# Window attention with its gradients: weight gradients in 64x64 array tiles between md and attention, scores two quads ahead

## The chip, the cores and the metric

One core of one Trainium2 chip. The metric is the device time of one execution in us; lower is better. Fast runs of one kernel mostly agree within 0.3%. A profile gives a trace of the engines: PE (TensorE matmul), PEld (its weight loads), DVE (VectorE), ACT (ScalarE), POOL (GpSimd), SP (SyncE, which issues DMA). Times read in the trace count from the start of the span, which is about 2 us shorter than the metric.

## The reference

Attention in 8x8 windows of a 256x256 image with 384 channels (one head), its output, and the gradients of x, wqkv and wo:

```
xw  = x in windows of 64 tokens                       # 1024 windows
q, k, v = split(xw @ wqkv)
p   = softmax(q k^T * C**-0.5)
o   = (p @ v) @ wo                                    # out_0
grads = vjp(f, x, wqkv, wo)(grad_out)                 # out_1, out_2, out_3
```

## The kernel before

The kernel handles eight windows at a time, a "quad": four tiles t of two windows each, 128 tokens in 128 partitions. There are 128 quads, unrolled. Names used below:

- *proj* makes YHT from X and DO with folded weights; *scores* are the window scores and their gradients; *chain* is softmax and its gradient, which give PB.
- *turn_p* turns PB on PE into TT; *md* multiplies X with TT into MD.
- *attention* multiplies PB with X and DO into VW (needed for weight gradients) and with YH into the first part of the gradient of x; *dxs* adds the second part, MD with AT_sb; *outs* is the output.
- *wgrad* multiplies X with VW of three quads at a time into weight gradients, 24 matmuls of 128x128 weights by 384 columns per quad.

PS is the whole PSUM: 8 banks of 512 columns; PSF is the same as 4096 columns, so column 2304 is column 256 of bank 4.

```python
    def attn_all(n, S):
        v = (n % NVW) * 4
        fvw = ((3072, 3584), (1536, 1920), (2304, 2688), (3072, 3584))
        for t in range(4):
            attn(n, t, 0, fvw[t][0], t * C)
            if t == 2:
                ev(ACT, VW[:, v + 1, ...], PSF[:, 1536:2304])   # cut: rearrange
            attn(n, t, 1, fvw[t][1], t * C)
            if t == 0:
                ev(ACT, VW[:, v, 0, :], PSF[:, 3072:3456])
                ev(DVE, VW[:, v, 1, :], PSF[:, 3584:3968])
        ev(DVE, VW[:, v + 2, ...], PSF[:, 2304:3072])
        # ... cut: turn_p, copies of t = 3

    def wgrad(g, k, bank):
        which, ma = k // CK, k % CK
        tiles = [(q, t) for q in groups[g] for t in range(4)]
        for i, (q, t) in enumerate(tiles):
            mm(PS[:, bank, 0:C], X[:, (q % NX) * 4 + t, ma * P:(ma + 1) * P], VW[:, (q % NVW) * 4 + t, which, :],
               i == 0, i == len(tiles) - 1)
        # ... cut: DVE adds the bank to ACC
```

`ev(engine, out, in)` is a copy out of PSUM. The copy of t=1 stands not after attention of t=1, but after the first part of t=2. Order on PE in a steady step: scores, md, wgrad, outs, wgrad, proj, attention, turn_p, dxs (t=0, 1), proj, dxs (t=2, 3).

Of the kernel before, what the change touches and what calls it, by code (L numbers as in the profile page):

```python
# [16 lines left out]
def kernel(  # L17
# [23 lines left out]
    NX, ND, NXT, NDT, NYH, NTOK, NVW = 11, 5, 3, 2, 2, 3, 6  # L41
# [33 lines left out]
    def mm(out, lhsT, rhs, start, stop):  # L75
        PE.matmul(out, lhsT=lhsT, rhs=rhs, start=start, stop=stop, skip_group_check=True)  # L76
# [50 lines left out]
    def scores(n):  # L127


        for m in range(CK):  # L130
            for w in range(2):
                for t in range(4):
                    mm(PS[:, 6, w * 256 + t * 64:w * 256 + t * 64 + 64],
                       HYS[:, m * 4 + t, 2 * w:2 * w + 2, :].rearrange("p b k -> p (b k)"),
                       XT[:, n % NXT, t * CK + m, w * 64:w * 64 + 64], m + w + t == 0, m == CK - 1)
# [3 lines left out]
    def sd(r, w):  # L139
        return PS[HALF[r], 6, w * 256:w * 256 + 256].rearrange("p (t k) -> p t k", t=4)  # L140
# [22 lines left out]
    def turn_p(n):  # L163
        for t in range(4):
            bb = PS[:, 6 + t // 2, C:512].bitcast(BF16)
            for a in range(2):
                for w in range(2):
                    r = slice(64 * w, 64 * w + 64)
                    o = (t % 2) * P + a * 64
                    PE.transpose(bb[r, o:o + 64], PB[r, n % 2, a, t, :], ident[r, r])  # L170

    def turn_p_ev(n):
        ev(DVE, TT[:, n % 2].rearrange("p (b t) a k -> p b (t a k)", b=2), PS[:, 6:8, C:512].bitcast(BF16))

    def md(n):
        for m in reversed(range(CK)):
            for t in range(4):
                for hh in range(2):
                    for w in range(2):
                        r = slice(64 * w, 64 * w + 64)  # L180
                        mm(PS[64 * hh:64 * hh + 64, 2 * m + w, t * P:t * P + P],
                           X[r, (n % NX) * 4 + t, m * P + hh * 64:m * P + hh * 64 + 64],
                           TT[r, n % 2, t, :, :], True, True)
            for w in range(2):
                dst = MD[:, m, :, 1:3, :] if w == 0 else MD[:, m, :, 0::3, :]
                ev(DVE if w == 0 and m > 0 else ACT, dst, PS[:, 2 * m + w, :].rearrange("p (t a k) -> p t a k", t=4, a=2))
# [37 lines left out]
    def attn_all(n, S):  # L224
        v = (n % NVW) * 4
        fvw = ((3072, 3584), (1536, 1920), (2304, 2688), (3072, 3584))
        for t in range(4):
            attn(n, t, 0, fvw[t][0], t * C)
            if t == 2:
                ev(ACT, VW[:, v + 1, :, :].rearrange("p a c -> p (a c)"), PSF[:, 1536:2304])  # L230
            attn(n, t, 1, fvw[t][1], t * C)
            if t == 0:
                ev(ACT, VW[:, v, 0, :], PSF[:, 3072:3456])
                ev(DVE, VW[:, v, 1, :], PSF[:, 3584:3968])
        ev(DVE, VW[:, v + 2, :, :].rearrange("p a c -> p (a c)"), PSF[:, 2304:3072])
        if S is not None:
            turn_p(S)
        ev(ACT, VW[:, v + 3, 0, :], PSF[:, 3072:3456])
        ev(DVE, VW[:, v + 3, 1, :], PSF[:, 3584:3968])
        if S is not None:  # L240
            turn_p_ev(S)

    def dxs(n, h):
        for t in (2 * h, 2 * h + 1):
            for m in range(CK):
                mmf(t * C, slice(0, P), MD[:, m, t, 0:2, :].rearrange("p a k -> p (a k)"),
                    lambda c0, c1: AT_sb[:, m, c0:c1], False, m == CK - 1)

    def dxs_ev(n, h, eng):
        ev(eng, DXS[:, n % 2, 2 * h:2 * h + 2, :].rearrange("p a c -> p (a c)"), PSF[:, 2 * h * C:2 * h * C + 2 * C])  # L250
        dxs_st(n, 2 * h)

    def dxs_st(n, t0):
        for t in range(t0, t0 + 2):
            for w in range(2):
                POOL.dma_start(out=img(out_1, n, t)[8 * w:8 * w + 8], in_=DXS[64 * (1 - w):64 * (1 - w) + 64, n % 2, t, :])  # L256

    def wgrad(g, k, bank):
        which, ma = k // CK, k % CK
        tiles = [(q, t) for q in groups[g] for t in range(4)]  # L260
        for i, (q, t) in enumerate(tiles):
            mm(PS[:, bank, 0:C], X[:, (q % NX) * 4 + t, ma * P:(ma + 1) * P], VW[:, (q % NVW) * 4 + t, which, :],
               i == 0, i == len(tiles) - 1)
        if g == 0:
            DVE.tensor_copy(out=ACC[:, k, :], in_=PS[:, bank, 0:C])
        else:
            DVE.tensor_tensor(out=GF[:, k, :] if g == len(groups) - 1 else ACC[:, k, :], in0=PS[:, bank, 0:C],
                              in1=ACC[:, k, :], op=ALU.add)
# [3 lines left out]
    def fill(*banks):  # L272

        left = 4 * GQ
        for b in banks:
            if todo and left >= 4 * len(groups[todo[0][0]]):
                g, k = todo.pop(0)
                wgrad(g, k, b)
                left -= 4 * len(groups[g])
# [19 lines left out]
    def step(n):  # L299
        T, S, A = n, n + 1, n + 2  # L300
        doT, doS, doA = 0 <= T < NQ, 0 < S < NQ, 0 < A < NQ
        early = not todo
        if 1 < n + 4 < NQ:
            load_do(SP, n + 4)
            load_x(POOL, n + 4)
        if 1 < n + 3 < NQ:
            turn_in(n + 3, 0)
            turn_in(n + 3, 1)
        if doS:
            scores(S)  # L310
        if doT:
            md(T)
        if doS:
            chain0(S)
        if early and doA:
            proj(A, 0, (7, 4, 5, 3), (ACT, ACT, ACT, DVE))
            turn_yh(A, 0)
        else:
            fill(7)
        if doS:  # L320
            chain2(S)
            chain3(S)
        if doT:
            outs(T, 0, 0, ACT)
            outs(T, 2, 2, ACT)
            outs_st(T)
        if not early:
            fill(7)
        if doA:
            proj(A, int(early), (3, 1, 2, 5), (ACT, ACT, ACT, DVE))  # L330
            turn_yh(A, int(early))
        else:
            fill(3, 1, 4)
        if doT:
            attn_all(T, S if doS else None)
        if doA:
            stack(A, 0, 0, 3)
            if early:
                stack(A, 1, 0, 3)
        if doT:  # L340
            dxs(T, 0)
            dxs_ev(T, 0, ACT)
        if doA and not early:
            proj(A, 1, (3, 4, 5, 7), (ACT, ACT, ACT, DVE))
            stack(A, 1, 0, 2)
            stack(A, 1, 2, 3)
            turn_yh(A, 1)
        elif not doA:
            fill(3, 4, 5)
        if doT:  # L350
            dxs(T, 1)
            dxs_ev(T, 1, ACT)
        elif S == 0:
            turn_p(S)
            turn_p_ev(S)
        g = [g for g in groups if g[-1] == n]
        if g:
            todo.extend((groups.index(g[0]), k) for k in range(2 * CK))
# [4 lines left out]
    with tc.manual_schedule():  # L363
# [3 lines left out]
        make_identity(nc, ident[:])  # L367
        for m in range(CK):
            SP.dma_start(out=w_sb[:, m, 0:2 * C], in_=wqkv[m * P:(m + 1) * P, 0:2 * C])
        ACT.activation(out=SS[:], in_=TM[:], func=ACTF.Exp)  # L370
        load_x(ACT, 0)
        POOL.dma_start(out=wo_sb[:], in_=wo.rearrange("(m p) n -> p m n", p=P))
        SP.dma_start(out=w_sb[:, :, 2 * C:], in_=wqkv.rearrange("(m p) j -> p m j", p=P)[:, :, 2 * C:])
        load_do(POOL, 0)
        turn_in(0, 0)
        turn_in(0, 1)
        load_x(SP, 1)
# [9 lines left out]

        for j in range(2 * CK):
            wturn(j, DVE if j % 2 == 0 else ACT)
        wprod(A_sb, wT[:, 0:CK], wT[:, CK:2 * CK], True)  # L390
        gate(A_sb[0:1, 2, 0:1])
        load_do(POOL, 1)
        turn_in(1, 0)
        turn_in(1, 1)
        for j in range(2 * CK, 3 * CK):
            wturn(j, DVE)
        proj(0, 0, (0, 1, 2, 3), (ACT, DVE, ACT, DVE))
        turn_yh(0, 0)
        wprod(BT_sb, wo_sb, wT[:, 2 * CK:3 * CK], False)
        gate(BT_sb[0:1, 2, 0:1])  # L400
        stack(0, 0, 0, 3)
        load_do(SP, 2)
        load_x(POOL, 2)
        proj(0, 1, (3, 4, 5, 7), (ACT, DVE, ACT, DVE))
        stack(0, 1, 0, 2)
        stack(0, 1, 2, 3)
        turn_yh(0, 1)
        scores(0)
        chain0(0)
        chain2(0)  # L410
        chain3(0)
        wprod(AT_sb, wT[:, CK:2 * CK], wT[:, 0:CK], True)
        wprod(B_sb, wT[:, 2 * CK:3 * CK], wo_sb, False)
        for n in range(-1, NQ):
# [76 lines left out]
```

## Time and profile before

| | before |
|---|---|
| median time | 1994.93 us (1993.6 to 1995.72) |
| PE busy | 99% of the span |
| ACT, DVE busy | 65%, 68% |
| one steady step, md to md | 15.16 us |
| md of quad 0 starts at | 35.6 us |
| PE's program (weight loads and matmuls, one row each) | 55044 rows |

A group's row of the profile has its count, then busy us and mean ns of one instruction, then idle time of the engine just before. The weight gradients on PE, with shapes kept apart:

```profile
L76 PE MATMUL PS<-VW,X 128*128 128x384 bf16 x3072 | 541.8, 326 | 0.0
```

And ACT's copies of VW:

```profile
L80 ACT CAST VW<-PS 128x384 bf16<-128x384 f32 x256 | 123.3, 482 | 16.8 <-PE PS L76 6.8
L80 ACT CAST VW<-PS 128x768 bf16<-128x768 f32 x128 | 102.3, 799 | 16.3 <-PE PS L76 0.6 <-DVE VW L82 0.3
```

The reader is to see that a matmul's 326 ns is its latency, not its cost (they start 162 ns apart), that nothing idles before weight gradients, and that only one tile in four is copied by ACT in one piece of 768 columns, 0.80 us.

### The profile page before, as it was taken

Reading aid. Unit: us, or ns where it says so; the run is one execution under the profiler, and the core shown is the slowest. Engines: PE = TensorE matmul, PEld = TensorE weight load, DVE = VectorE, ACT = ScalarE, POOL = GpSimd, SP = SyncE. Lnnn points to the kernel's source line nnn. Section 1 sums busy time; section 2 is a strip of 40 time slices with the busy share of each in tenths; the row PEclk is TensorE's granted clock in tenths of the full one; section 3 lists DMA queues with packets and bytes.
Section 4 is the critical chain, followed back from the end, with each engine's and each line's share of the span. In section 5 each row is a group of like instructions: output and inputs, shape, how many; then the busy total and the mean of one; then the engine's idle time right before and its main releaser. Section 6 shows DMA issues by size and latency. Waiting matters only on the chain.

```text
span 1992.9 us, 68590 instructions
## 1 busy us (share of the span) xinstructions
PE 1965.5 (99%) x27521; PEld 1312.0 (66%) x27521; DVE 1346.8 (68%) x2971; ACT 1301.9 (65%) x2323; POOL 1295.0 (65%) x2313
## 2 busy tenths in 40 slices
PE   6999999999999999999999999999999999999999
PEld 3666666666666666666666666666666666666665
DVE  4676666667666666766666676666667666666765
ACT  3766666666666666666666666666666666666664
POOL 3766666666666666666666666666666666666753
PEclk8999999999999999999999999999999999999999
DMA  9999999999999999999999999999999999999993
GB/s 185 229 202 222 206 217 210 212 204 214 201 220 206 211 207 215 209 212 208 210 208 215 206 212 206 214 210 206 205 218 209 208 215 209 207 214 208 214 168 83
DMA packets 978559, 410.17 MB, mean 206 GB/s; under 512 B 861568, under 2 KB 953600, under 8 KB 978240
## 3 DMA queue, kind: packets, MB, share of 16 engines
q1 hardware_dynamic: 878880, 253.43, 78.6%
q0 software_dynamic: 98384, 151.68, 29.0%
q8 instruction: 215, 3.52, 0.7%
q14 instruction: 104, 0.85, 0.2%
q10 hardware_dynamic: 976, 0.69, 0.1%
HBM read 101.84 MB, written 101.84 MB: 102 GB/s over the span
## 4 chain that ended last, share of the span: by engine, by line
PE 97%; DMA 2%; ACT 1%; DVE 0%; POOL 0%; issue 0%; ACTq 0%; DVEq 0%; SPq 0%
PE PS L76 95%; PE PS L170 2%; DMA X<-in_x_dram 1%; DMA XT<-X 1%; DMA out_dram<-DXS 0%; ACT DXS L80 0%; ACT VW L428 0%; POOL X L94 0%; ACT OS L80 0%; DVE BT_sb L297 0%; ACT YHT L80 0%; POOL out_dram L256 0%; ACTq L94 0%; ACT MD L80 0%; DVE ST L144 0%
## 5 line engine op out<-in xcount | busy, mean ns | idle before, releaser
L256 POOL DMA_DIRECT2D out_dram<-DXS x1024 | 578.6, 571 | 411.1 <-ACT DXS L80 373.7
L76 PE MATMUL PS<-VW,X 128*128 128x384 bf16 x3072 | 541.8, 326 | 0.0
L80 ACT CAST YHT<-PS 128x256 bf16<-128x256 f32 (+1 forms) x766 | 369.9, 518 | 251.4 <-PE PS L76 234.5
L76 PEld LDWEIGHTS <-X 64*64 64x64 bf16 (+1 forms) x9216 | 380.4, 103 | 201.2 <-issue 1.0
L76 PEld LDWEIGHTS <-MD 128*128 128x128 bf16 x3840 | 338.2, 98 | 151.2 <-issue 3.5
L80 ACT CAST DXS<-PS 128x768 bf16<-128x768 f32 x256 | 204.6, 799 | 195.3 <-PE PS L76 187.6
L82 DVE CAST VW<-PS 128x384 bf16<-128x384 f32 (+1 forms) x384 | 253.3, 687 | 94.7 <-ACT VW L80 91.7
L82 DVE CAST YHT<-PS 128x256 bf16<-128x256 f32 (+1 forms) x258 | 110.0, 426 | 290.4 <-PE PS L76 283.5
L76 PE MATMUL PS<-AT_sb,MD 128*128 128x384 bf16 (+2 forms) x2304 | 294.7, 273 | 2.7 <-ACT DXS L80 2.7
L80 ACT CAST MD<-PS 128x512 bf16<-128x512 f32 x512 | 263.1, 599 | 51.9 <-PE PS L76 51.8
L94 POOL DMA_DIRECT2D X<-in_x_dram x504 | 269.6, 547 | 30.9 <-DMA out_dram<-DXS 20.0
L197 POOL DMA_DIRECT2D out_dram<-OS x512 | 277.6, 550 | 11.9 <-ACT VW L80 9.4
L76 PE MATMUL PS<-XT,A_sb 128*128 128x512 bf16 (+1 forms) x1536 | 273.6, 328 | 10.1 <-DMA XT<-X 10.1
L76 PE MATMUL PS<-DOT,BT_sb 128*128 128x512 bf16 (+1 forms) x1536 | 270.8, 326 | 4.5 <-ACT OS L80 2.7
L76 PE MATMUL PS<-B_sb,MD 128*128 128x384 bf16 x1536 | 270.5, 326 | 0.0
L82 DVE CAST MD<-PS 128x512 bf16<-128x512 f32 x256 | 165.0, 685 | 143.4 <-PE PS L76 143.4
L80 ACT CAST VW<-PS 128x384 bf16<-128x384 f32 (+1 forms) x384 | 212.4, 587 | 33.2 <-PE PS L76 7.4
L76 PEld LDWEIGHTS <-A_sb 128*128 128x128 bf16 x1536 | 151.0, 98 | 125.1 <-issue 13.5
L80 ACT CAST OS<-PS 128x768 bf16<-128x768 f32 x256 | 204.6, 799 | 24.3 <-PE PS L76 18.2
L76 PEld LDWEIGHTS <-BT_sb 128*128 128x128 bf16 x1536 | 150.2, 98 | 104.0 <-issue 4.8
L160 POOL TENSOR_TENSOR UM<-PB,ST 128x256 f32<-128x256 bf16 x128 | 78.5, 613 | 207.2 <-DVE ST L159 203.3
L76 PE MATMUL PS<-YH,PB 64*64 64x256 bf16 (+2 forms) x3072 | 194.4, 273 | 0.0
(59 smaller groups left out, 1979.5 us busy)
## 6 DMA issues: line engine op xcount, KB each, us to landing
out_dram<-OS POOLq DMA_DIRECT2D x512, 96.0 KB, 4.4
out_dram<-DXS POOLq DMA_DIRECT2D x1024, 48.0 KB, 4.1
X<-in_x_dram POOLq DMA_DIRECT2D x504, 96.0 KB, 5.0
DO<-in_grad_out_dram SPq DMA_DIRECT2D x504, 96.0 KB, 4.3
YH<-YHT SPq DMA_TRANSPOSE x256, 5.3
XT<-X SPq DMA_TRANSPOSE x128, 6.2
DOT<-DO SPq DMA_TRANSPOSE x128, 6.2
DO<-in_grad_out_dram POOLq DMA_DIRECT2D x8, 96.0 KB, 4.0
```

The source lines that it names most:

```text
L76: PE.matmul(out, lhsT=lhsT, rhs=rhs, start=start, stop=stop, skip_group_check=True)
L80: ACT.copy(out=out, in_=in_)
L82: DVE.tensor_copy(out=out, in_=in_)
L94: q.dma_start(out=X[:, (n % NX) * 4 + t, :], in_=img(x, n, t))
L160: POOL.tensor_tensor(out=UM[:], in0=pb[:, 1], in1=bcast(3), op=ALU.mult)
L170: PE.transpose(bb[r, o:o + 64], PB[r, n % 2, a, t, :], ident[r, r])
L197: POOL.dma_start(out=img(out_0, n, t), in_=OS[:, n % 2, t, :])
L256: POOL.dma_start(out=img(out_1, n, t)[8 * w:8 * w + 8], in_=DXS[64 * (1 - w):64 * (1 - w) + 64, n % 2, t, :])
```

## The change

Intent: PE is the bound, and what it loses are its changes between 128x128 and 64x64 tiling. If the weight gradients run as 64x64 tiles too, and stand between md and the halves of attention, which are 64x64 already, two of four changes a step go. To make room, scores run two quads ahead, the first four quads are turned on PE and not by DMA, all copies of VW go to ACT, and the PSUM banks are dealt anew. The core of the diff:

```diff
-    def attn_all(n, S):
-        ...
+    DXB = 5 * 512
+    def attn2(n, h, fv):
+        v = (n % NVW) * 4
+        for t in (2 * h, 2 * h + 1):
+            f = fv[t % 2]
+            attn(n, t, 0, f, DXB + t * C)
+            attn(n, t, 1, f + C, DXB + t * C)
+            ev(ACT, VW[:, v + t, :, :].rearrange("p a c -> p (a c)"), PSF[:, f:f + 2 * C])

     wgrad:
+            for hh in range(2):
+                for w in range(2):
+                    r, o = slice(64 * w, 64 * w + 64), slice(64 * hh, 64 * hh + 64)
+                    mm(PS[o, banks[w], 0:C], X[r, xs, ma * P + hh * 64:ma * P + hh * 64 + 64], VW[r, vs, which, :], s0, s1)

     step (quad n; S = n + 2, A = n + 3), steady case:
+        md(n)
+        wgrad(g, k, (4, 7)); wgrad_add(g, k, (4, 7))
+        attn2(n, 0, (0, 2 * C))
+        stack(S, ...)
+        wgrad(g, k, (3, 4)); turn_p(n + 1); wgrad_add(g, k, (3, 4))
+        attn2(n, 1, (0, 2 * C))
+        dxs(n, 0); dxs(n, 1); scores(S); chain0(S); dxs(n, 3); dxs_ev(n, 0, ACT); dxs(n, 2)
+        chain2(S); dxs_ev(n, 1, ACT); chain3(S)
+        proj(A, 0, (0, 1, 2, 4), ...); outs(...); proj(A, 1, (7, 2, 4, 3), ...)
```

More of the change, by code (lines that the diff above doesn't have):

```diff
@@ L40 @@
     groups += [(q,) for q in range(len(groups) * GQ, NQ)]
-    NX, ND, NXT, NDT, NYH, NTOK, NVW = 11, 5, 3, 2, 2, 3, 6
+    NX, ND, NXT, NDT, NYH, NTOK, NVW = 11, 6, 3, 2, 2, 3, 6
+    PTURN = 4
     PE, DVE, ACT, POOL, SP = nc.tensor, nc.vector, nc.scalar, nc.gpsimd, nc.sync
@@ L132, in scores @@
                 for t in range(4):
-                    mm(PS[:, 6, w * 256 + t * 64:w * 256 + t * 64 + 64],
+                    mm(PS[:, 3, w * 256 + t * 64:w * 256 + t * 64 + 64],
                        HYS[:, m * 4 + t, 2 * w:2 * w + 2, :].rearrange("p b k -> p (b k)"),
@@ L139, in sd @@
     def sd(r, w):
-        return PS[HALF[r], 6, w * 256:w * 256 + 256].rearrange("p (t k) -> p t k", t=4)
+        return PS[HALF[r], 3, w * 256:w * 256 + 256].rearrange("p (t k) -> p t k", t=4)
     def chain0(n):
@@ L163, in turn_p @@
     def turn_p(n):
+        bb = PS[:, 2, 256:512].bitcast(BF16)
         for t in range(4):
-            bb = PS[:, 6 + t // 2, C:512].bitcast(BF16)
             for a in range(2):
@@ L168, in turn_p, with pturn, pturn_in @@
                     r = slice(64 * w, 64 * w + 64)
-                    o = (t % 2) * P + a * 64
+                    o = t * P + a * 64
                     PE.transpose(bb[r, o:o + 64], PB[r, n % 2, a, t, :], ident[r, r])
-    def turn_p_ev(n):
-        ev(DVE, TT[:, n % 2].rearrange("p (b t) a k -> p b (t a k)", b=2), PS[:, 6:8, C:512].bitcast(BF16))
+        DVE.tensor_copy(out=TT[:, n % 2, :, :, :].rearrange("p t a k -> p (t a k)"), in_=bb)
+    def pturn(dst, src, banks, engs):
+        for h in range(2):
+            pt = PS[:, banks[h], :].bitcast(BF16)
+            for i in range(6):
+                PE.transpose(pt[:, i * P:(i + 1) * P], src(6 * h + i), ident[:])
+            ev(engs[h], dst[:, 6 * h:6 * h + 6, :].rearrange("p j k -> p (j k)"), pt[:, 0:6 * P])
+    def pturn_in(n, a, banks, engs):
+        nat = X[:, (n % NX) * 4:(n % NX) * 4 + 4, :] if a == 0 else DO[:, (n % ND) * 4:(n % ND) * 4 + 4, :]
+        pturn(XT[:, n % NXT] if a == 0 else DOT[:, n % NDT],
+              lambda j: nat[:, j // CK, (j % CK) * P:(j % CK + 1) * P], banks, engs)
+    MB = ((2, 3), (1, 6), (0, 5))
     def md(n):
@@ L180, in md @@
                         r = slice(64 * w, 64 * w + 64)
-                        mm(PS[64 * hh:64 * hh + 64, 2 * m + w, t * P:t * P + P],
+                        mm(PS[64 * hh:64 * hh + 64, MB[m][w], t * P:t * P + P],
                            X[r, (n % NX) * 4 + t, m * P + hh * 64:m * P + hh * 64 + 64],
@@ L185, in md @@
                 dst = MD[:, m, :, 1:3, :] if w == 0 else MD[:, m, :, 0::3, :]
-                ev(DVE if w == 0 and m > 0 else ACT, dst, PS[:, 2 * m + w, :].rearrange("p (t a k) -> p t a k", t=4, a=2))
+                ev(DVE if w == 0 else ACT, dst, PS[:, MB[m][w], :].rearrange("p (t a k) -> p t a k", t=4, a=2))
     def outs(n, t0, b0, eng):
@@ L222, in attn @@
             c = e
-    def attn_all(n, S):
+    DXB = 5 * 512
+    def attn2(n, h, fv):
         v = (n % NVW) * 4
-        fvw = ((3072, 3584), (1536, 1920), (2304, 2688), (3072, 3584))
-        for t in range(4):
-            attn(n, t, 0, fvw[t][0], t * C)
-            if t == 2:
-                ev(ACT, VW[:, v + 1, :, :].rearrange("p a c -> p (a c)"), PSF[:, 1536:2304])
-            attn(n, t, 1, fvw[t][1], t * C)
-            if t == 0:
-                ev(ACT, VW[:, v, 0, :], PSF[:, 3072:3456])
-                ev(DVE, VW[:, v, 1, :], PSF[:, 3584:3968])
-        ev(DVE, VW[:, v + 2, :, :].rearrange("p a c -> p (a c)"), PSF[:, 2304:3072])
-        if S is not None:
-            turn_p(S)
-        ev(ACT, VW[:, v + 3, 0, :], PSF[:, 3072:3456])
-        ev(DVE, VW[:, v + 3, 1, :], PSF[:, 3584:3968])
-        if S is not None:
-            turn_p_ev(S)
@@ L243, in dxs @@
-    def dxs(n, h):
-        for t in (2 * h, 2 * h + 1):
-            for m in range(CK):
-                mmf(t * C, slice(0, P), MD[:, m, t, 0:2, :].rearrange("p a k -> p (a k)"),
-                    lambda c0, c1: AT_sb[:, m, c0:c1], False, m == CK - 1)
+        for t in (2 * h, 2 * h + 1):
+            f = fv[t % 2]
+            attn(n, t, 0, f, DXB + t * C)
+            attn(n, t, 1, f + C, DXB + t * C)
+            ev(ACT, VW[:, v + t, :, :].rearrange("p a c -> p (a c)"), PSF[:, f:f + 2 * C])
@@ L249, in dxs_ev, with dxs @@
+    def dxs(n, t):
+        for m in range(CK):
+            mmf(DXB + t * C, slice(0, P), MD[:, m, t, 0:2, :].rearrange("p a k -> p (a k)"),
+                lambda c0, c1: AT_sb[:, m, c0:c1], False, m == CK - 1)
     def dxs_ev(n, h, eng):
-        ev(eng, DXS[:, n % 2, 2 * h:2 * h + 2, :].rearrange("p a c -> p (a c)"), PSF[:, 2 * h * C:2 * h * C + 2 * C])
-        dxs_st(n, 2 * h)
-    def dxs_st(n, t0):
-        for t in range(t0, t0 + 2):
+        ev(eng, DXS[:, n % 2, 2 * h:2 * h + 2, :].rearrange("p a c -> p (a c)"),
+           PSF[:, DXB + 2 * h * C:DXB + 2 * h * C + 2 * C])
+        for t in (2 * h, 2 * h + 1):
@@ L255, in dxs_st, with wgrad_add @@
             for w in range(2):
                 POOL.dma_start(out=img(out_1, n, t)[8 * w:8 * w + 8], in_=DXS[64 * (1 - w):64 * (1 - w) + 64, n % 2, t, :])
-    def wgrad(g, k, bank):
+    def wgrad_add(g, k, banks):
+        for i, b in enumerate(banks):
+            if g == 0 and i == 0:
+                DVE.tensor_copy(out=ACC[:, k, :], in_=PS[:, b, 0:C])
+            else:
+                last = g == len(groups) - 1 and i == len(banks) - 1
+                DVE.tensor_tensor(out=GF[:, k, :] if last else ACC[:, k, :], in0=PS[:, b, 0:C], in1=ACC[:, k, :], op=ALU.add)
@@ L259, in wgrad @@
+    def wgrad(g, k, banks):
         which, ma = k // CK, k % CK
@@ L261, in wgrad @@
         for i, (q, t) in enumerate(tiles):
-            mm(PS[:, bank, 0:C], X[:, (q % NX) * 4 + t, ma * P:(ma + 1) * P], VW[:, (q % NVW) * 4 + t, which, :],
-               i == 0, i == len(tiles) - 1)
-        if g == 0:
-            DVE.tensor_copy(out=ACC[:, k, :], in_=PS[:, bank, 0:C])
-        else:
-            DVE.tensor_tensor(out=GF[:, k, :] if g == len(groups) - 1 else ACC[:, k, :], in0=PS[:, bank, 0:C],
-                              in1=ACC[:, k, :], op=ALU.add)
+            s0, s1 = i == 0, i == len(tiles) - 1
+            xs, vs = (q % NX) * 4 + t, (q % NVW) * 4 + t
+            if len(banks) == 1:
+                mm(PS[:, banks[0], 0:C], X[:, xs, ma * P:(ma + 1) * P], VW[:, vs, which, :], s0, s1)
+                continue
+            for hh in range(2):
+                for w in range(2):
+                    r, o = slice(64 * w, 64 * w + 64), slice(64 * hh, 64 * hh + 64)
+                    mm(PS[o, banks[w], 0:C], X[r, xs, ma * P + hh * 64:ma * P + hh * 64 + 64], VW[r, vs, which, :], s0, s1)
     todo = []
@@ L277, in fill @@
                 g, k = todo.pop(0)
-                wgrad(g, k, b)
+                wgrad(g, k, (b,))
+                wgrad_add(g, k, (b,))
                 left -= 4 * len(groups[g])
@@ L299, in step @@
     def step(n):
-        T, S, A = n, n + 1, n + 2
-        doT, doS, doA = 0 <= T < NQ, 0 < S < NQ, 0 < A < NQ
+        S, A = n + 2, n + 3
+        doS, doA = S < NQ, A < NQ
         early = not todo
-        if 1 < n + 4 < NQ:
-            load_do(SP, n + 4)
-            load_x(POOL, n + 4)
-        if 1 < n + 3 < NQ:
-            turn_in(n + 3, 0)
-            turn_in(n + 3, 1)
+        if n + 5 < NQ:
+            load_do(SP, n + 5)
+            load_x(POOL, n + 5)
+        if PTURN <= n + 4 < NQ:
+            turn_in(n + 4, 0)
+            turn_in(n + 4, 1)
@@ new lines, in step @@
+        md(n)
+        if early:
+            if doA:
+                if A < PTURN:
+                    pturn_in(A, 0, (4, 7), (DVE, DVE))
+                    pturn_in(A, 1, (4, 7), (DVE, DVE))
+                proj(A, 0, (7, 4, 0, 5), (ACT, ACT, ACT, DVE))
+                proj(A, 1, (3, 7, 4, 6), (ACT, ACT, ACT, DVE))
+            if doS:
+                stack(S, 0, 0, 3)
+                stack(S, 1, 0, 3)
+            if n + 1 < NQ:
+                turn_p(n + 1)
+            attn2(n, 0, (0, 2 * C))
+            attn2(n, 1, (3 * 512, 0))
+            if doA:
+                turn_yh(A, 0)
+                turn_yh(A, 1)
+        else:
+            g, k = todo.pop(0)
+            wgrad(g, k, (4, 7))
+            wgrad_add(g, k, (4, 7))
+            attn2(n, 0, (0, 2 * C))
+            if doS:
+                stack(S, 0, 0, 3)
+                stack(S, 1, 0, 3)
+            g, k = todo.pop(0)
+            wgrad(g, k, (3, 4))
+            if n + 1 < NQ:
+                turn_p(n + 1)
+            wgrad_add(g, k, (3, 4))
+            attn2(n, 1, (0, 2 * C))
@@ L309, in step @@
+        dxs(n, 0)
+        dxs(n, 1)
         if doS:
             scores(S)
-        if doT:
-            md(T)
-        if doS:
             chain0(S)
-        if early and doA:
-            proj(A, 0, (7, 4, 5, 3), (ACT, ACT, ACT, DVE))
-            turn_yh(A, 0)
-        else:
-            fill(7)
+        dxs(n, 3)
+        dxs_ev(n, 0, ACT)
+        dxs(n, 2)
         if doS:
             chain2(S)
+        dxs_ev(n, 1, ACT)
+        if doS:
             chain3(S)
-        if doT:
-            outs(T, 0, 0, ACT)
-            outs(T, 2, 2, ACT)
-            outs_st(T)
@@ L327, in step @@
-        if not early:
-            fill(7)
-        if doA:
-            proj(A, int(early), (3, 1, 2, 5), (ACT, ACT, ACT, DVE))
-            turn_yh(A, int(early))
-        else:
-            fill(3, 1, 4)
-        if doT:
-            attn_all(T, S if doS else None)
-        if doA:
-            stack(A, 0, 0, 3)
-            if early:
-                stack(A, 1, 0, 3)
-        if doT:
-            dxs(T, 0)
-            dxs_ev(T, 0, ACT)
-        if doA and not early:
-            proj(A, 1, (3, 4, 5, 7), (ACT, ACT, ACT, DVE))
-            stack(A, 1, 0, 2)
-            stack(A, 1, 2, 3)
+        if doA and not early:
+            proj(A, 0, (0, 1, 2, 4), (ACT, ACT, ACT, DVE))
+            turn_yh(A, 0)
+        elif not doA:
+            fill(0, 1, 2)
@@ L347, in step @@
+        outs(n, 0, 5, ACT)
+        outs(n, 2, 0, ACT)
+        outs_st(n)
+        if doA and not early:
+            proj(A, 1, (7, 2, 4, 3), (ACT, ACT, ACT, DVE))
             turn_yh(A, 1)
         elif not doA:
-            fill(3, 4, 5)
-        if doT:
-            dxs(T, 1)
-            dxs_ev(T, 1, ACT)
-        elif S == 0:
-            turn_p(S)
-            turn_p_ev(S)
+            fill(7, 2, 4)
         g = [g for g in groups if g[-1] == n]
@@ L367 @@
         make_identity(nc, ident[:])
+        load_x(ACT, 0)
         for m in range(CK):
             SP.dma_start(out=w_sb[:, m, 0:2 * C], in_=wqkv[m * P:(m + 1) * P, 0:2 * C])
+        load_do(SP, 0)
+        ACT.dma_start(out=w_sb[:, :, 2 * C:], in_=wqkv.rearrange("(m p) j -> p m j", p=P)[:, :, 2 * C:])
+        ACT.dma_start(out=wo_sb[:], in_=wo.rearrange("(m p) n -> p m n", p=P))
         ACT.activation(out=SS[:], in_=TM[:], func=ACTF.Exp)
-        load_x(ACT, 0)
-        POOL.dma_start(out=wo_sb[:], in_=wo.rearrange("(m p) n -> p m n", p=P))
-        SP.dma_start(out=w_sb[:, :, 2 * C:], in_=wqkv.rearrange("(m p) j -> p m j", p=P)[:, :, 2 * C:])
-        load_do(POOL, 0)
-        turn_in(0, 0)
-        turn_in(0, 1)
-        load_x(SP, 1)
+        gate(w_sb[0:1, 2, 0:1])
+        for n in (1, 2):
+            load_x(POOL, n)
+            load_do(POOL, n)
+        load_do(SP, 3)
+        load_x(POOL, 3)
+        load_do(SP, 4)
+        load_x(POOL, 4)
         for i in range(12):
@@ L386, in wturn @@
             ev(eng, wT[:, j, :], pt[:, 0:C])
+        pturn_in(0, 0, (6, 7), (DVE, ACT))
         for j in range(2 * CK):
@@ L390 @@
         wprod(A_sb, wT[:, 0:CK], wT[:, CK:2 * CK], True)
-        gate(A_sb[0:1, 2, 0:1])
-        load_do(POOL, 1)
-        turn_in(1, 0)
-        turn_in(1, 1)
         for j in range(2 * CK, 3 * CK):
             wturn(j, DVE)
+        pturn_in(0, 1, (6, 7), (DVE, DVE))
         proj(0, 0, (0, 1, 2, 3), (ACT, DVE, ACT, DVE))
@@ L399 @@
         wprod(BT_sb, wo_sb, wT[:, 2 * CK:3 * CK], False)
-        gate(BT_sb[0:1, 2, 0:1])
         stack(0, 0, 0, 3)
-        load_do(SP, 2)
-        load_x(POOL, 2)
-        proj(0, 1, (3, 4, 5, 7), (ACT, DVE, ACT, DVE))
-        stack(0, 1, 0, 2)
-        stack(0, 1, 2, 3)
+        pturn_in(1, 0, (6, 7), (ACT, ACT))
+        proj(0, 1, (4, 5, 0, 1), (ACT, DVE, ACT, DVE))
+        stack(0, 1, 0, 3)
         turn_yh(0, 1)
+        pturn_in(1, 1, (6, 7), (ACT, ACT))
         scores(0)
         chain0(0)
+        proj(1, 0, (0, 1, 2, 4), (ACT, ACT, ACT, ACT))
+        turn_yh(1, 0)
         chain2(0)
         chain3(0)
+        proj(1, 1, (5, 6, 7, 0), (ACT, ACT, ACT, ACT))
+        turn_yh(1, 1)
+        stack(1, 0, 0, 3)
+        stack(1, 1, 0, 3)
         wprod(AT_sb, wT[:, CK:2 * CK], wT[:, 0:CK], True)
+        scores(1)
+        chain0(1)
         wprod(B_sb, wT[:, 2 * CK:3 * CK], wo_sb, False)
-        for n in range(-1, NQ):
+        pturn_in(2, 0, (6, 7), (ACT, DVE))
+        pturn_in(2, 1, (6, 7), (ACT, DVE))
+        turn_p(0)
+        chain2(1)
+        chain3(1)
+        proj(2, 0, (0, 1, 4, 5), (ACT, ACT, ACT, ACT))
+        turn_yh(2, 0)
+        proj(2, 1, (6, 7, 0, 4), (ACT, ACT, ACT, ACT))
+        turn_yh(2, 1)
+        for n in range(NQ):
             step(n)
```

## The prediction

> **What bounds the kernel now.** I read the totals of the profile first, then the chain that ended last, then the order of time on PE in the middle of the run.
>
> ```profile
> PE 1965.5 (99%) x27521; PEld 1312.0 (66%) x27521; DVE 1346.8 (68%) x2971; ACT 1301.9 (65%) x2323; POOL 1295.0 (65%) x2313
> ...
> PE 97%; DMA 2%; ACT 1%; DVE 0%; POOL 0%; issue 0%; ACTq 0%; DVEq 0%; SPq 0%
> ```
>
> PE is busy 99% of the span and carries 97% of the chain; the other engines have a third of the span free. So whatever PE gains or waits shows in the time. One steady step (one quad of window pairs; there are 128), from the timeline of PE:
>
> ```profile
> 1017.74 0.43 PE L170 MATMUL PS<-ident,PB 64*64 64x64 bf16 x16
> 1018.11 1.16 PE L76 MATMUL PS<-AT_sb,MD 128*128 128x384 bf16 x9
> 1019.10 2.11 PE L76 MATMUL PS<-DOT,BT_sb 128*128 128x512 bf16 x12
> 1021.05 1.15 PE L76 MATMUL PS<-AT_sb,MD 128*128 128x256 bf16 x9
> 1022.06 0.87 PE L76 MATMUL PS<-XT,HYS 128*128 128x64 bf16 x24
> 1022.87 0.86 PE L76 MATMUL PS<-TT,X 64*64 64x128 bf16 x48
> 1023.66 2.12 PE L76 MATMUL PS<-VW,X 128*128 128x384 bf16 x12
> 1025.63 2.11 PE L76 MATMUL PS<-B_sb,MD 128*128 128x384 bf16 x12
> 1027.58 2.11 PE L76 MATMUL PS<-VW,X 128*128 128x384 bf16 x12
> 1029.53 2.11 PE L76 MATMUL PS<-XT,A_sb 128*128 128x512 bf16 x12
> 1031.57 0.35 PE L76 MATMUL PS<-X,PB 64*64 64x384 bf16 x2
> ```
>
> First column is the start. No row carries an idle bracket: PE never waits. From one md (the 48 matmuls of TT and X) to the next I read 15.16 us, the same to 0.01 in over 120 steps on end. md of quad 0 starts at 35.6 us, the first step takes 20.5, the next two 13.35 (no weight gradients yet), and after the last md 30.3 us remain.
>
> What is left to gain on PE is the change between 128x128 and 64x64 tiles. The two projections have the same twelve matmuls, yet the one before dxs takes 1.95 (1019.10 to 1021.05) and the one before attention 2.04 (1029.53 to 1031.57). Read one start at a time, the last matmul there holds its place for 203 ns instead of 109, and the first group of tiles takes 24 ns more than a later one: 0.12 us. The same reading gives 0.12 from scores to md (123 ns for 29, then 80 for 56), 0.11 from md to weight gradients, 0.11 from turned P to dxs. Four changes a step, 0.46 us.
>
> **What the Trainium skill says.** "TensorEngine Tiling (Array Packing)", Key Properties, says a change of tiling mode drains TensorE; the 0.11 to 0.12 us above agree. "TensorE: Matmul & The Clock Gate", Part 3, says tiles at different positions run at once, starting about 4 ns apart: in this trace four tiles of attention start 3 to 4 ns apart, and a group of four with 384 columns takes 162 ns, exactly what one 128x128 matmul of 384 columns takes here. "PSUM — Partial Sum Buffer", PSUM bank collisions, says that two engines must not touch one bank and quadrant at once, whatever the columns, so software keeps them apart by bank. The trace agrees that waits go by bank:
>
> ```profile
> DVE VW L82 <- ACT VW L80: 91.7, 128, 1.1
> ```
>
> This is DVE's copy of columns 2304 to 3071, waiting once a step, 0.72 us each, for ACT's copy of 1536 to 2303: no column is shared, only bank 4. And PE meets it in an early step:
>
> ```profile
> 52.30 1.16 PE L76 MATMUL PS<-AT_sb,MD 128*128 128x384 bf16 x9
> 54.34 1.14 PE L76 MATMUL PS<-AT_sb,MD 128*128 128x256 bf16 x9 [0.89 <-ACT DXS L80]
> ```
>
> The first half of dxs fills columns 0 to 767, ACT copies them out (768 columns, 799 ns in the row of this copy below), the second half begins at 768, in the same bank 1, and stands 0.89 us after the modelled end of the matmul before. Start to start it is 1.159 us where 0.109 is usual, so **1.05 us of PE are lost**: 0.20 from the end of streaming to ACT's start, 0.80 copy, 0.05 back. In steady steps a projection lies between the halves and hides this.
>
> ```profile
> L80 ACT CAST DXS<-PS 128x768 bf16<-128x768 f32 x256 | 204.6, 799 | 195.3 <-PE PS L76 187.6
> ```
>
> **The change part by part.**
>
> 1. *Weight gradients in 64x64 tiles.* 24 matmuls of 128x128 a step become 96 of 64x64, four at a time: 12 x 162 ns twice, 3.9 us before and after. The four loads of 64 columns stay hidden, as they do in md, whose groups of four follow each other in 56 ns. Each result lies in two banks, so DVE adds twice: about 250 more adds of 0.56 us, +140 us of DVE.
>
> 2. *Order.* md, weight gradients, attention half, weight gradients, turned P, attention half are now all 64x64; dxs, scores, dxs, proj, outs, proj are 128x128. Two changes of mode in place of four: 0.114 + 0.118 = **-0.23 us** a step.
>
> 3. *Copies of VW.* All go to ACT as 768 columns: attention's t=0 writes columns 0 to 767, t=1 768 to 1535, t=2 and t=3 likewise. ACT copies each straight after. Column 768 is in bank 1, which ACT is still reading. The built program confirms it: the first matmul of t=1 (bank 1, column 256) waits for ACT's copy of t=0, and the first of t=3 for that of t=2. Nothing stands between on PE, and PE keeps its order. ACT is free at both points, so each costs the 1.05 us above: **+2.10 us** a step. The kernel before avoided this by having ACT copy t=1 only after the first part of t=2 had passed the shared bank.
>
> 4. *md's new banks.* Its third part writes bank 3, which the DVE copy of the last projection piece still holds: from that piece's start 0.317 to DVE, 0.425 copy, 0.05 back = 0.79 us; PE would be there at 0.68. **+0.11**. Other new waits (wgrad on banks 4 and 7, scores on bank 3, outs on bank 6) I walked with the durations of this trace: all end before PE arrives, outs by only 0.1.
>
> 5. *More splits in attention, dxs after scores:* I choose **+0.03**.
>
> Period: 15.16 - 0.23 + 2.10 + 0.11 + 0.03 = **17.17 us**, 2.01 more, for 122 steps (quads 3 to 124): +245 us.
>
> 6. *Ends.* Before md(0), two transposed loads off the chain (PE waited 4.5 and 5.5 us for them, the second inside the first step), but PE turns these quads itself (96 transposes of about 60 ns, 6 us) and projects quad 2 earlier. I put md(0) at 38 us (+2.5) and the first step, which also turns quad 3 with DVE copies in between, at 20 (-0.5). Steps 1 and 2: one stall of 1.05, one of about 0.55: +3. The last three steps: +5.5 of waits and changes less 3.9 for a projection moved ahead: +1.6.
>
> Sum: 1994.9 + 245 + 6.6 = 2246.5, say **2247 us**.
>
> **Rivals.** *The stalls are hidden and only the changes of mode count.* Then 122 x (-0.23 + 0.14) = -11, with about -2 at the ends, gives some 1982, or 1965 without the +0.14. For it: this is surely the intent. Against it: the wait is in the built program and the early step shows its size. If only one of the two stands, about 2120. *ACT or DVE becomes the bound.* ACT loses 256 copies of 384 (123 us), 128 of MD (about 77) and gains 384 of 768 (307): 1302 + 107 = 1409 us. DVE loses 264 us of VW, gains 140 and 128 MD copies of 0.69 (88): about 1311. Both far under 2247; no bound, but a copy late on ACT would lengthen each stall. *Tiled weight gradients run slower than one wide matmul*, by their loads or two banks at once: each 10% is 0.39 us a step, +48 us. md and attention at full rate speak against it. *DMA.* It is at nine tenths or more throughout; the bytes stay and the step gets longer, so it gets easier.
>
> **Range and chances.** Each 0.1 us of a stall is 25 us in all; startup is known to 5, unforeseen waits may add 0.3 a step (37), and my walk may have placed bank 3 wrongly (-14). So 2205 to 2290. Faster by over 2% needs both stalls absent: 2%. Within 2%: 3%. Slower: 95%.
>
> **What would show it.** PE's timeline should show two idle brackets of 0.89 us from ACT VW in each step, about 215 to 225 us in the list of waits, and PE's busy share down to 88 or 89%; from md to md 17.2 us; no gap between md, weight gradients and attention; weight gradients at 1.95 us per twelve groups; the ACT row of VW with 512 copies of 0.80 us. I am wrong if PE runs past the copy, if weight-gradient groups take more than 165 ns, or if md(0) comes after 45 us.

## The result, and the profile after

The changed kernel takes 2252.05 us in the median (2251.83 to 2252.19, 4 runs) against 1994.26 of the kernel before in the same rounds: ratio 1.1292, 95% interval 1.1273 to 1.1312, slower. Ratios and intervals are those from fast runs of the same rounds alone, so not quite the ratios of the medians. Executions over 1.5% slower than the fastest of the same kernel are left out of the means. All outputs are right. The granted clock was 1.0 in the profile, 0.997 in that of the kernel before.

The totals and the chain, as before:

```profile
PE 2000.6 (89%) x38665; PEld 1492.2 (66%) x38665; DVE 1315.4 (58%) x2846; ACT 1387.7 (62%) x2334; POOL 1295.7 (58%) x2315
...
PE 88%; ACT 10%; issue 1%; DVE 1%; DMA 0%; ACTq 0%; POOL 0%; DVEq 0%
PE PS L77 86%; ACT VW L81 9%; PE PS L171 1%; ACT DXS L81 0%; DMA out_dram<-DXS 0%; DMA X<-in_x_dram 0%; ACT OS L81 0%; DVE HYS L126 0%; ACT VW L474 0%; PE PS L179 0%; DVE SS L147 0%; DVE ST L145 0%; ACT YHT L81 0%; ACTq L95 0%; DVE MD L83 0%
```

PE fell from 99% to 89%, and a new member stands in the chain: ACT's copy of VW, 9% of the span, some 200 us, though ACT is busy for less of the span than before. PE's own list of waits names it too:

```profile
PE PS L77 <- ACT VW L81: 226.0, 257, 0.9
```

257 waits are two for each quad and one. Where they stand, from the timeline of PE in one steady step:

```profile
1068.03 1.00 PE L77 MATMUL PS<-TT,X 64*64 64x128 bf16 x48
1068.82 2.16 PE L77 MATMUL PS<-VW,X 64*64 64x384 bf16 x48
...
1070.98 0.27 PE L77 MATMUL PS<-DO,PB 64*64 64x128 bf16 x2
...
1072.19 0.24 PE L77 MATMUL PS<-X,PB 64*64 64x128 bf16 x2 [0.89 <-ACT VW L81]
...
1072.52 2.15 PE L77 MATMUL PS<-VW,X 64*64 64x384 bf16 x48
...
1076.13 0.30 PE L77 MATMUL PS<-X,PB 64*64 64x256 bf16 x2 [0.89 <-ACT VW L81]
...
1076.59 1.16 PE L77 MATMUL PS<-AT_sb,MD 128*128 128x384 bf16 x9
1077.58 0.86 PE L77 MATMUL PS<-XT,HYS 128*128 128x64 bf16 x24
```

The first bracket stands at the first matmul of t=1, the second at that of t=3. ACT's side of the same stretch shows the two copies that end them:

```profile
1071.34 0.80 ACT L81 CAST VW<-PS 128x768 bf16<-128x768 f32 x1 [1.20 <-PE PS L77]
1072.75 0.80 ACT L81 CAST VW<-PS 128x768 bf16<-128x768 f32 x1 [0.61 <-PE PS L77]
1075.29 0.80 ACT L81 CAST VW<-PS 128x768 bf16<-128x768 f32 x1 [1.74 <-PE PS L77]
```

ACT starts on t=0 at 1071.34 and ends at 1072.14; PE starts t=1 at 1072.19. ACT and PE take turns, each idle while the other works: ACT was idle for 1.20 us before its copy. The weight gradients themselves cost what they did:

```profile
L77 PE MATMUL PS<-VW,X 64*64 64x384 bf16 x12000 | 538.8, 322 | 0.0
```

12000 small matmuls and 72 wide ones (from step 126 on) are busy for 538.8 and 12.5 us where 3072 wide ones were for 541.8.

One steady step by stage, each the time from its first matmul to the next stage's first, so a change of tiling mode falls to the stage before it:

| stage, us | before | after |
|---|---|---|
| md | 0.797 | 0.788 |
| two weight gradients | 3.911 | 3.900 |
| attention and turn_p | 1.700 | 3.873 |
| dxs | 2.008 | 1.976 |
| scores | 0.804 | 0.699 |
| two proj | 3.993 | 3.994 |
| outs | 1.950 | 1.950 |
| step | 15.163 | 17.180 |

All of the loss lies in attention. Of its +2.173 us, 2.094 are the two waits (start to start, 1.047 each). The other stages together gained 0.156 us.

### The profile page after: what moved, and what is told of

It is laid out like the page before. It is cut to its first block, busy times and chain, and to the rows that moved or that the text cites. A ratio compares the mean times of both kernels' runs of the same rounds, so it can differ in the third digit from the quotient of the medians.

```text
span 2250.2 us, 90611 instructions
## 1 busy us (share of the span) xinstructions
PE 2000.6 (89%) x38665; PEld 1492.2 (66%) x38665; DVE 1315.4 (58%) x2846; ACT 1387.7 (62%) x2334; POOL 1295.7 (58%) x2315
## 4 chain that ended last, share of the span: by engine, by line
PE 88%; ACT 10%; issue 1%; DVE 1%; DMA 0%; ACTq 0%; POOL 0%; DVEq 0%
PE PS L77 86%; ACT VW L81 9%; PE PS L171 1%; ACT DXS L81 0%; DMA out_dram<-DXS 0%; DMA X<-in_x_dram 0%; ACT OS L81 0%; DVE HYS L126 0%; ACT VW L474 0%; PE PS L179 0%; DVE SS L147 0%; DVE ST L145 0%; ACT YHT L81 0%; ACTq L95 0%; DVE MD L83 0%
## 5 line engine op out<-in xcount | busy, mean ns | idle before, releaser
L81 ACT CAST VW<-PS 128x768 bf16<-128x768 f32 x512 | 408.0, 798 | 521.5 <-PE PS L77 519.8
L77 PEld LDWEIGHTS <-X 64*64 64x64 bf16 x18216 | 531.8, 107 | 69.9 <-issue 29.3
L77 PE MATMUL PS<-VW,X 64*64 64x384 bf16 (+1 forms) x12072 | 551.3, 323 | 0.0
L77 PE MATMUL PS<-X,PB 64*64 64x128 bf16 (+1 forms) x2042 | 184.8, 245 | 224.4 <-ACT VW L81 224.3
L77 PEld LDWEIGHTS <-PB 64*64 64x64 bf16 x8192 | 190.8, 106 | 272.2 <-issue 270.7
L81 ACT CAST YHT<-PS 128x512 bf16<-128x512 f32 (+1 forms) x770 | 359.0, 523 | 9.7 <-PE PS L77 7.8
L267 DVE TENSOR_TENSOR ACC<-PS,ACC 128x384 f32<-128x384 f32 x502 | 278.8, 555 | 110.9 <-PE PS L77 93.3
L77 PE MATMUL PS<-YH,PB 64*64 64x128 bf16 (+2 forms) x4096 | 265.2, 247 | 0.0
L145 DVE TENSOR_REDUCE ST<-PS 64x4 f32<-64x256 f32 x256 | 108.1, 422 | 260.9 <-PE PS L77 256.9
L83 DVE CAST MD<-PS 128x512 bf16<-128x512 f32 x384 | 241.5, 684 | 7.4 <-PE PS L77 7.4
```

What stands on the lines that cost most here:

```text
L77: PE.matmul(out, lhsT=lhsT, rhs=rhs, start=start, stop=stop, skip_group_check=True)
L81: ACT.copy(out=out, in_=in_)
L83: DVE.tensor_copy(out=out, in_=in_)
L145: DVE.tensor_reduce(out=ST[HALF[w], 0, :], in_=sd(w, w), axis=AX.X, op=ALU.max)
L267: DVE.tensor_tensor(out=GF[:, k, :] if last else ACC[:, k, :], in0=PS[:, b, 0:C], in1=ACC[:, k, :], op=ALU.add)
```

## The experiments

All edits are against the changed kernel unless said otherwise. Each was run beside the kernel before on the same chip.

**1. The copy one part later.** In each half of attention ACT copies the first tile only after the first part of the second has passed the shared bank 1.

```diff
         attn(n, t, 0, f, ...); attn(n, t, 1, f + C, ...)
-        ev(ACT, VW of t)
         attn(n, t + 1, 0, g, ...)
+        ev(ACT, VW of t)
         attn(n, t + 1, 1, g + C, ...)
         ev(ACT, VW of t + 1)
```

> The changed kernel, but ACT copies t=0 (and t=2) only after the first part of t=1 (t=3) has passed bank 1, as the kernel before ordered it. Theory (PE stands 1.05 us twice a step for ACT's copy in the shared bank): both waits vanish, and two short ones come out that they hid: 0.15 us at the second weight gradient for DVE's add in bank 4, 0.23 us at t=3 for DVE's copy of TT in bank 2. Period 17.18 - 2.09 + 0.38 = 15.47 us, in all about 2035 us. Rival (tiled weight gradients with twice the adds, or the wide copies on ACT, are slow in themselves): the time stays over 2200 us.

Measured: 2063.16 us (4 runs), ratio 1.0342 to the kernel before: 189 us of the 258 lost came back with one moved line per half. The list of waits of PE:

```profile
PE PS L77 <- ACT VW L81: 1.6, 4, 0.6
```

From 226.0 to 1.6 us; the four that stay stand in the start and the first three steps. So the order of the copy is the cause. The rival, that tiles or the wide copies are slow in themselves, falls: both are still there. The size was 28 us off. The steady step is 15.60 us, not 15.47: the wait at bank 4 came out as expected (wgrad 2.091 for 1.950), but turn_p after it takes 0.31 us up to its 13th transpose where it took 0.19. In the single starts, the four tiles are out of step after that wait; I did not test whether that is the reason. Some 8 us more lie in single steps that are longer than the rest; experiment 6 is about those.

**2. The same in the first half alone.** The edit of experiment 1 in `attn2(n, 0, ...)` only.

> The late copy in the first half of attention alone. Theory: each wait counts by itself; one of 1.05 us goes, 0.15 us for bank 4 comes out: period 16.29 us, about 2141 us. Rival (the second wait takes over what the first gave up): about 2250 us.

Measured: 2148.69 us (one run, state unknown; its period of 16.35 us is the better number). One wait is gone and the other is unchanged: PE waits 112.4 us for ACT VW, 129 times. Each wait counts by itself; the rival falls.

**3. Short copy first.** The banks and the order on PE stay. ACT's copy of the first tile is cut in two, the part in the shared bank first.

```diff
-            ev(ACT, VW of t, PSF[:, f:f + 768])
+            ev(ACT, last 256 columns, the part in bank 1)
+            ev(ACT, first 512 columns, bank 0)
```

(For the second tile the copy stays whole. In the first three steps the half at column 1536 is cut likewise.)

> The changed kernel, but ACT's copy of t=0 and t=2 is cut in two, the 256 columns in bank 1 first, the 512 in bank 0 after. The banks and the order on PE stay. Theory (PE waits for the length of the instruction that reads the shared bank): each wait falls from 0.20 + 0.80 + 0.05 to 0.20 + 0.38 + 0.05 us, so the bracket before t=1 from 0.89 to 0.47; period 16.34 us, about 2148 us. Rival (PE waits for the whole copy of t=0, or for ACT's load, which grows by 512 instructions' fixed cost): 2250 us or more.

Measured: 2149.39 us (4 runs), ratio 1.0773. PE's timeline, the two brackets of a step:

```profile
1025.07 0.24 PE L77 MATMUL PS<-X,PB 64*64 64x128 bf16 x2 [0.46 <-ACT VW L81]
...
1028.59 0.30 PE L77 MATMUL PS<-X,PB 64*64 64x256 bf16 x2 [0.46 <-ACT VW L81]
```

And the copies:

```profile
L81 ACT CAST VW<-PS 128x512 bf16<-128x512 f32 x256 | 151.5, 592 | 0.0
L81 ACT CAST VW<-PS 128x256 bf16<-128x256 f32 x256 | 95.4, 373 | 368.0 <-PE PS L77 364.6 <-PE PS L171 3.5
```

The bracket shrank by 0.43 us (0.89 to 0.46), as the copy that holds the bank did (798 to 373 ns), although ACT now works longer in all. PE waits for the instruction that reads the shared bank and for nothing else. The period, 16.33 us, is the 16.34 expected.

**4. The same fault put into the kernel before.** 128x128 weight gradients, old order; the copy of t=1 moved ahead of the first part of t=2.

```diff
-            attn(n, t, 0, fvw[t][0], t * C)
-            if t == 2:
-                ev(ACT, VW of t = 1, PSF[:, 1536:2304])
-            attn(n, t, 1, fvw[t][1], t * C)
+            attn(n, t, 0, fvw[t][0], t * C)
+            attn(n, t, 1, fvw[t][1], t * C)
+            if t == 1:
+                ev(ACT, VW of t = 1, PSF[:, 1536:2304])
```

> The kernel before, but ACT copies t=1 at once, ahead of the first part of t=2, which shares bank 4 with it. 128x128 weight gradients, all else as before. Theory: one wait of about 1.1 us a step appears (0.06 of it because ACT is still copying t=0): period 16.27 us, about 2135 us. Rival (the loss belongs to the tiles or to the order of scores, not to the order of the copy): it stays at 1994 us.

Measured: 2128.08 us (4 runs), ratio 1.0670; the step is 16.22 us.

```profile
PE PS L76 <- ACT VW L80: 113.3, 128, 0.9
```

One wait a step of 0.89 us in a kernel that has nothing else of the change. Moving one line costs this tuned kernel 133 us. The expected extra 0.06 us for a busy ACT did not show.

**5. Late copy, weight gradients wide again.** Experiment 1 with each weight gradient as 12 matmuls of 128x128 into one bank (banks 4 and 3), one add.

> As the first experiment (late copy), but each weight gradient is 12 matmuls of 128x128 into one bank, with one add. Against that experiment it undoes the tiles alone. Theory: four more changes of tiling mode a step at 0.115 us each, +0.46, less the 0.15 us wait for bank 4, which two banks per result had made: period 15.78 us, about 2073 us. Rival A (the tiles bring nothing, their loads and adds cost as much): as the first experiment, 2035. Rival B (tiles are slower): below 2035.

Measured: 2080.85 us (4 runs), ratio 1.0432, so 18 us slower than experiment 1 on the medians. The steady step is 15.82 us against 15.60 with tiles. By stages: md 0.932 for 0.788, the weight gradients 4.106 for 4.041, the first half of attention 0.787 for 0.660. So the tiles do save time, 0.22 us of a step, less than the expected 0.31, because experiment 1 was slower than expected. In all it is less than 0.22 times 122 steps, because experiment 1 has the irregular steps and this has almost none (0.7 us against 7.8, worked out as below). The two ran on different chips, where the kernel before had the same median, 1995.5 us. Both rivals fall.

**6. The bared waits moved away.** Experiment 1, and:

```diff
-            wgrad(g, k, (3, 4)); turn_p(n + 1)
+            wgrad(g, k, (3, 4), with turn_p(n + 1) before its 11th of 12 groups)
-            proj(A, 1, (7, 2, 4, 3), (ACT, ACT, ACT, DVE))
+            proj(A, 1, (7, 2, 3, 4), (ACT, ACT, ACT, DVE))
     first steps only:
+            dxs_ev(n, 1, ACT) before chain2(S), not after
```

> Late copy, and the short waits that it bares taken out too: P turned after 10 of the 12 tile groups of the second weight gradient, so that TT is copied before t=3 needs bank 2; the last two pieces of the second projection swap banks 3 and 4, so that md need not wait for DVE; in the first steps the second dxs copy ahead of the exponential. Only the 0.15 us wait for bank 4 stays. Theory: period 15.47 - 0.23 - 0.09 = 15.15 us, about 1991 us, within 1% of the kernel before: the -0.23 us of saved mode changes is all but used up by that wait and by splits. Rival (the new order itself costs more): over 2010 us.

Measured: 2006.38 us (6 runs, 2002.72 to 2011.02), ratio 1.0064. The steady step is 15.08 us, a little better than expected (15.15), and md is down to 0.694. Yet it is 15 us slower than expected; two of the six runs were over the rival's 2010 us. Most steps take 15.08 us, but some up to 17.1. I took, for quads 4 to 123, each stage's time less its median over the steps, and summed: 18.1 us, against 0.0 in the kernel before, 0.8 in the changed one and 7.8 in experiment 1. The longest, from the timeline of PE (the column after the start is the time up to the last end of the merged run):

```profile
199.69 0.83 PE L77 MATMUL PS<-XT,HYS 128*128 128x64 bf16 x23
202.39 0.19 PE L77 MATMUL PS<-XT,HYS 128*128 128x64 bf16 x1 [1.87 <-issue]
```

PE does 23 of 24 scores matmuls and then stands for 1.87 us. "issue" means that no semaphore and no transfer in the profile ended it. The list of waits:

```profile
PE PS L77 <- issue: 10.3, 20, 1.9
```

In the trace, these 20 gaps and one more of 0.6 us in turn_p end 1.2 to 2.3 us after the end of a 16 KB transfer on a queue that loads instructions, all but one within 1.8 us, though such a transfer ends only every 6.3 us (median). These are PE's own: 302 of them for 77332 rows (weight loads and matmuls, one row each), 215 in the kernel before for 55044, 256 rows each. Four of them (us):

```
last load of instructions    gap of PE
119.72 to 120.68             121.78 to 122.11
199.81 to 200.98             200.52 to 202.39
626.04 to 627.02             627.58 to 628.52
1625.80 to 1626.75           1627.10 to 1628.21
```

That looks like a PE that has run out of instructions: the tiles raised its program from 55044 rows to 77332. Experiments 7 and 8 test it.

**7. Fewer pieces.** Experiment 6, but attention cuts each of its two outputs at its own bank border; before, both were cut wherever either had one. Same columns, 48 matmuls of attention a step in place of 64.

```diff
-        ends = [c for c in range(P, C, P) if (fv + c) % 512 == 0 or (fdx + c) % 512 == 0] + [C]
-        (each piece: two matmuls into VW's banks, two into dx's)
+        for k, f in ((0, fv), (1, fdx)): cuts of this output alone
+        (pieces of both outputs in order of their first column)
```

> As the sixth experiment, but attention cuts its two outputs each at its own bank border and not both at either's: 48 matmuls of attention a step in place of 64, so 73236 rows in PE's program in place of 77332, the same columns. The sixth showed a steady step of 15.08 us, but some steps up to 2 us longer, 18 us in all, in gaps of PE that no semaphore ends, each 1.4 to 2.3 us after a 16 KB load of instructions. Theory (PE runs dry of instructions, because the tiles raised its instructions per us and the DMA queues are full): the steady step stays 15.08, the irregular excess falls to under half, about 1994 us. Rival (the gaps are refresh or DMA accidents that have nothing to do with the number of instructions): 2006 us.

Measured: 1992.15 us in the median of six runs: four of 1988.26 to 1992.19, one of 2015.2, one slow of 2027.84. Ratio 1.0011, interval 0.9973 to 1.0050: the same as the kernel before, though four of the runs lie below its fastest run beside them, 1993.7. In the profile, which is of the fastest run, the steady step stays at 15.08 us, the irregular part is 3.5 us for 18.1, and:

```profile
PE PS L77 <- issue: 1.8, 4, 0.6
```

4096 rows less took most of the gaps away in this run, and four of the six times agree, as the theory asked. The runs of 2015.2 and 2027.84 are slower than any of experiment 6 and were not profiled; what they lost stays open.

**8. More rows in the kernel before.** Its weight gradients, outs and projections cut into matmuls of 128 columns.

```diff
-            mm(PS[:, bank, 0:C], X tile, VW[..., :], ...)
+            for c in range(0, C, P):
+                mm(PS[:, bank, c:c + P], X tile, VW[..., c:c + P], ...)
     (outs and proj likewise)
```

> The kernel before with its 128x128 weight gradients, outs and projections cut into matmuls of 128 columns: same order, waits, tiling modes and results, but 85764 rows in PE's program in place of 55044. By the 56 ns that a 128-column matmul takes in place of a third of 162 or a quarter of 216, the steady step grows by 0.32 us to 15.48, in all about 2034 us. Theory (PE runs dry of instructions): on top of it irregular gaps without a releaser, over 18 us in all, so over 2050. Rival (the gaps belong to 64x64 tiles): none, 2034 us.

Measured: 2036.99 us (4 runs), ratio 1.0210 (1.0196 to 1.0223). The steady step is 15.46 us, as expected. Gaps without a releaser did appear:

```profile
PE PS L76 <- issue: 5.1, 7, 1.8
```

They stand in a kernel without tiled weight gradients, and each ends 1.2 to 1.6 us after a load of instructions, so the tiles are not needed for them. But the irregular part is 7.8 us, not over 18, although this kernel has the most rows per us of all: 85764 in 2039 us, 42, against 38.6 in experiment 6 (77332 in 2002). The other kernels with tiled weight gradients, one profile each, have 0.8 us at 34.4 rows per us (the changed one), 1.8 and 5.2 at 36.0 (experiments 2 and 3), 3.5 at 36.9 (7), 7.8 at 37.5 (1) and 18.1 at 38.6 (6): among them it grows, roughly, with rows per us, and experiment 8 lies off that line. So the number of rows matters but does not settle how much is lost. What else does, such as how the rows bunch within a step or when the DMA queues are full, stays open.

## Why the prediction was right

- *PE is the bound, so what it waits shows in full.* It held. PE at 89% is inside the forecast "88 or 89%", and the 257 us are PE's.
- *The two waits, 1.05 us each (part 3).* 1.047 measured, the bracket 0.89 as in the early step it was read from. This step carried the forecast, and experiments 1 to 4 show its mechanism: it goes with the order, halves with one half, follows the length of the copy, and can be planted in the kernel before. The list of waits has 226.0 us, just above the forecast 215 to 225.
- *Changes of mode, -0.23 (part 2).* The stages other than attention gained 0.156 in spite of a new wait of 0.094 in md, so 0.25 without it. 0.22 of that lies where the two changes went (scores, md, the weight gradient after md); the 0.03 in dxs is not explained.
- *Bank 3 at md, +0.11 (part 4).* md was 0.788 us; with the banks swapped (experiment 6) it was 0.694. So 0.094.
- *Splits, +0.03 (part 5).* This was a chosen number. What is left of attention is 2.173 - 2.094 = 0.08.
- *Period.* 2.094 + 0.094 - 0.25 + 0.08 = 2.02 us more; 17.18 measured, 17.17 forecast. That it fits to 0.01 is in part luck: the splits were 0.05 too small, the other three terms together 0.04 too high. From quad 3 to quad 125 the time grew by 246.7 us, forecast 245.
- *Tiled weight gradients at the rate of wide ones (part 1).* 1.950 us per twelve groups, no slower. ACT and DVE did not become the bound: 1387.7 and 1315.4 us busy, forecast 1409 and 1311.
- *Ends (part 6), +6.6 forecast, +10.6 measured.* md of quad 0 came at 37.3 us (38 forecast), the first step took 19.5 (20). Steps 1 and 2 took 15.87 and 15.75, not 14.85, and the last three steps with the end cost 5.0 us more, not 1.6. The missed piece is one wait: without a projection between dxs and outs, outs stand 1.67 us for the second dxs copy, which ACT does only after the exponential. The walk of part 4 covered steady steps alone. This wait stands in the first three steps and, with 1.60 us, in step 125. Experiment 6, whose first steps differ from those of experiment 1 only in the place of that copy, made steps 1 and 2 1.4 and 1.3 us shorter; with the one in step 125, which no run took away, it can account for most of the 5 us between 2247 and 2252.

What the prediction did not see, because the two waits hid it, is that the better order would have gained next to nothing: with all those waits moved, experiment 6 still did not beat the kernel before. Of the saved 0.23 us a step its steady step keeps 0.08; the rest goes to the wait for bank 4 (0.14 us in experiment 1), which two banks per weight gradient bring, and to attention's splits, and the irregular steps (18.1 us) take more than 0.08 a step gives. With fewer pieces (experiment 7) it drew level.

## What to carry to other kernels

When outputs of two tiles share a PSUM bank, in these programs the copy of the first stops the matmuls of the second until the instruction that reads the shared bank is done, even with no column in common (1.05 us here for 768 columns); put the copy after the second tile's passage through that bank, or read the shared bank first in a short instruction. Before judging a new order of a kernel whose bound has no gaps, walk every bank once through the new order: who read it last, and is the reader done when PE comes back. And count instructions as well as columns: quartering a matmul cost no array time here (1.950 us per twelve groups either way), but it may use up the slack of the instruction supply, as experiments 6 and 7 suggest.

## What the Trainium skill lacked or had wrong

- "TensorEngine Tiling (Array Packing)", Key Properties, says that a change of mode drains TensorE, without a cost. Here it is 0.11 to 0.12 us each way at a granted clock of 1.0, and taking the tiles out again (experiment 5) made the step 0.22 us longer.
- "PSUM — Partial Sum Buffer", PSUM bank collisions, gives the rule to guard by bank but no price. Here the turn PE to ACT and back costs 1.05 us with a copy of 768 columns: 0.20 to ACT's start, 0.80, 0.05 back; 0.62 with 256 columns.
- "Runtime: NRT & Kernel Launch", Instruction fetch mechanics, calls the crossing of a 16 KiB block of instructions mostly hidden. The loads in these traces are 16 KB each as it says, and in the kernel before they are hidden (irregular part 0.0 us); in experiment 6, 20 gaps of PE of up to 1.9 us, 10.3 us in all, end 1.2 to 2.3 us after such a load, and the irregular part is 18.1 us. No page says when they stop being hidden in unrolled code like this; neither do these runs.
- "TensorE: Matmul & The Clock Gate", Back-to-back issue gap, gives about 131 ns per matmul of 512 columns and about 81 for 128 columns as the sustained pace of load and matmul pairs. Here such pairs follow each other in 216 ns for 512 columns (the projections) and 56 for 128 (experiment 8), at a granted clock of 1.0.
